# Agent attention with a cosine feed-forward: a PSUM bank of its own for the output products, the program order kept on four engines, and the side work laid out by hand in half lots

## The chip, the cores and the metric

One core of a Trainium2 chip runs the kernel. The metric is the device time of one execution in microseconds (us). The engines are TensorE (PE in the profile, PEld for its weight loads), VectorE (DVE), ScalarE (ACT), GpSimd (POOL) and SyncE (SP), which issues the DMAs.

## The reference

Four batches of 12480 tokens with 128 channels, 49 agents, and a feed-forward of 2048 columns:

```
scale = 1 / sqrt(128)
sm(a, b) = softmax over the last axis of scale * (a @ b.T)
agent_v = sm(agents, k) @ v              # 49 x 128 per batch
x       = sm(q, agents) @ agent_v        # 12480 x 128 per batch
h       = x @ w_in                       # 49920 x 2048
out     = (h * cos(h)) @ w_out           # 49920 x 128
```

All of it is in float32. The kernel folds agent_v @ w_in into one matrix `a` per batch (`project`), so that h is softmax weights times `a`, and it computes h * (cos(h) - 1) and adds the linear part x @ w_in @ w_out by two short products (`project_out`, b1 and b2).

## The kernel before

**Work and names.** A group is 960 tokens (8 tiles of 120), 13 groups make a batch, 52 the whole. The feed-forward of a group takes two halves of 480 tokens with eight steps each, so 16 steps a group, 208 a batch (called a stretch here) and 832 in all, in the loop at line 512. One step n has four parts: two products on PE (L520) that fill a tile `ph` of two PSUM banks (three such tiles); the sine on ACT (L523) from `ph` to `c`, with the bias read from a tile `half_pi`; on DVE (c - 1) * h (L525) into `r`; and, four steps later (LAG), two products of `r` with w_out on PE (L542) that add up over eight steps in one PSUM bank. At the end of the eight come the two linear products (L538, L539), and ACT copies the bank to `osb` (L544), from where SP writes the output.

**Side work.** While the loop runs over one batch, the next batch is prepared, and so are the softmax weights of the groups that come. The side work goes by lots, one group each: a key lot (`Agents.scores`: eight products, L93, then an ACT copy L171 and a running maximum on DVE, L182), a query lot (`query`: eight products, L93, then DVE takes the maximum, L342, and subtracts it, L349), a values lot (`values`: eight products, L232). An fp32 product is two matmuls in the trace, so a lot of eight shows as 16. A query group is turned by four transposes (`query_turned`, L372, ACT copy L374, POOL L377 and L378). `Agents.shift` subtracts the maximum on POOL (L210). Once the keys and queries of a batch are in, ACT changes its function table from sine to exponential, takes the exponentials of all 13 key lots (three instructions, L214) and of all 13 query groups (three instructions, L353), and changes back: this is a burst. DVE then sums the queries' exponentials (`query_sums`, L357 to L359). Batch 0 has two small bursts of five groups, batches 1 to 3 a large one each.

**What sets the order.** All these one-bank results (scores, turned weights, the output products) come from one pool `p1` of two PSUM banks (`small`, the name `one` in the profile). `extra` gives a lot to a whole step, steps 1, 3 and 5 of eight; the lots of the next batch follow one another as early as they can, all keys, then all queries, then the burst, then all values. Only some instructions are pinned (`tc.keep_in_program_order`); the rest is put in order on each engine by a list scheduler.

Of the kernel before, what the change touches and what calls it, by code (L numbers as in the profile page):

```python
# [18 lines left out]
P = 128  # L19
# [16 lines left out]
LAG = 4  # L36
PAD = 64
# [4 lines left out]
def agent_attention_cos_ffn(ctx, tc, qT, kT, v, agT, w_in, w_out, outT):  # L42
# [15 lines left out]

    const = ctx.enter_context(tc.tile_pool(name="const", bufs=1))
# [4 lines left out]
    nc.gpsimd.memset(ones, 1.0)  # L64
    half_pi = const.tile([P, 1], F32, name="half_pi")
    nc.gpsimd.memset(half_pi, HALF_PI)
# [20 lines left out]
    def scores(sb, src, b, ps):  # L87

        xt = sb.tile([P, GRP], F32, name="xt", bufs=3)
        load(xt, src)  # L90
        ps = ps[:TT, :GT * NA].rearrange("p (t a) -> p t a", a=NA)
        for t in range(GT):
            nc.tensor.matmul(ps[:, t, :], xt[:, t * TT:(t + 1) * TT], ag[:, b, :], start=True, stop=True)  # L93
        return ps

    def scores_twice(xt, src, b, ps):
# [3 lines left out]
        for t in range(GT):  # L100
            nc.tensor.matmul(ps[:, t // HT, t % HT], xt[:, t * TT:(t + 1) * TT], twice(ag[:, b, :]),  # L101
                             start=True, stop=True)
        return ps[:, :, :, 0, :]

    class Weights:
# [6 lines left out]
        def single(self, src, out):  # L112
# [5 lines left out]
            nc.vector.tensor_scalar(ex, hi, 20, 0x7FF, op0=ALU.logical_shift_right, op1=ALU.bitwise_and)  # L118
            nc.vector.tensor_scalar(man, hi, 0xFFFFF, 0x100000, op0=ALU.bitwise_and, op1=ALU.bitwise_or)
            nc.vector.tensor_scalar(ex, ex, 1151.0, 896.0, op0=ALU.min, op1=ALU.max)  # L120
            f = man.bitcast(F32)
            nc.vector.scalar_tensor_tensor(f, lo, 2.0 ** -32, man, op0=ALU.mult, op1=ALU.add)
            nc.vector.tensor_scalar(ex, ex, 896.0, 2.0 ** 23, op0=ALU.subtract, op1=ALU.mult)
            nc.vector.scalar_tensor_tensor(f, f, 2.0 ** -20, ex.bitcast(F32), op0=ALU.mult, op1=ALU.mult)
            nc.vector.scalar_tensor_tensor(out.bitcast(U32), hi, 0x80000000, man, op0=ALU.bitwise_and, op1=ALU.bitwise_or)
# [5 lines left out]
        def w_out(self, c):  # L131
# [3 lines left out]
            nc.scalar.copy(w1[:, fs], w)  # L135
            return w

        def product(self, c, w, po, wio):

            pt = self.psum()  # L140
            for t in range(4):
                f = slice((4 * c + t) * P, (4 * c + t + 1) * P)
                nc.tensor.transpose(pt[:, t * P:(t + 1) * P], win[:, f], ident)
            wt = self.sb.tile([P, 4, P], F32, name="wt", bufs=2)
            nc.scalar.copy(wt.rearrange("p f d -> p (f d)"), pt)
            for t in range(4):
                nc.tensor.matmul(po, wt[:, t], w[:, t], start=(c == t == 0), stop=(4 * c + t == NF - 1))
            if 4 * c + 4 == NF:
                nc.vector.tensor_copy(wio, po)

    class Agents:
# [6 lines left out]
        def scores(self, g):  # L158
            sb = self.sb
            if g == 0:  # L160
# [5 lines left out]
                nc.gpsimd.memset(av[:, NA:HI], 0.0)  # L166
# [3 lines left out]
            if self.wide is None:  # L170
                nc.scalar.copy(s, scores(sb, src, self.b, self.psum()))  # L171
            else:
# [5 lines left out]
                nc.scalar.copy(s.rearrange("p (h t) a -> p h t a", h=2), ps)  # L178
            if g == 0:
                nc.vector.tensor_copy(self.run, s)  # L180
            else:
                nc.vector.tensor_max(self.run, self.run, s)  # L182
# [41 lines left out]
        def values(self, g):  # L224
            vt = self.sb.tile([TT, GT, P], F32, name="vt", bufs=4)
# [468 lines left out]
```

## Time and profile before

| | us |
|---|---|
| median of three timed runs (1282.61 to 1286.02) | 1284.95 |
| span of the profiled execution | 1283.9 |
| PE, PEld busy | 1188.2, 955.3 |
| DVE, ACT, POOL busy | 1087.6, 1005.6, 313.8 |

The span runs from the first to the last instruction of the profiled execution, and is the only time of that execution that is given; the median of the timed runs lies 1.05 above it. PE's busy time counts each matmul from its start to its modelled end, and pipelined matmuls overlap, so that how much of PE is used is read from the distance of starts, not from the busy share. The first output step's DVE instruction starts at 86.9, the last at 1274.8; ahead of that stand the loading of the weights and the keys and values of batch 0.

### The profile page before, as it was taken

How to read it: one execution, taken by the hardware profiler on the slowest of the kernel's cores; microseconds unless marked ns; L12 is line 12 of the kernel's file. 1: busy time of each engine (PE TensorE's matmuls, PEld its weight loads, DVE VectorE, ACT ScalarE, POOL GpSimd, SP SyncE). 2: the span in 40 equal slices, each digit the busy share in tenths (PEclk: the TensorE clock that was granted, in tenths of full speed). 3: DMA queues.
4: the chain of work that ended last, by engine and by line, in shares of the span. 5: the costliest groups of instructions: out<-in, count | busy, mean ns of one | idle time of the engine just before them, and what ended most of it. 6: DMA issues, size and time to landing. Idle time of an engine off the chain costs nothing.

```text
span 1283.9 us, 17193 instructions
## 1 busy us (share of the span) xinstructions
PE 1188.2 (93%) x6349; PEld 955.3 (74%) x6349; DVE 1087.6 (85%) x1214; ACT 1005.6 (78%) x1115; POOL 313.8 (24%) x341
## 2 busy tenths in 40 slices
PE   8799899996999999969999999996999999999997
PEld 8777787775987887758966788775986666666664
DVE  5878778887779888878799988787789999999997
ACT  2347778667779887676799988667789999999997
POOL 1201221415213115133132121415133122222220
PEclk9989999998999999999999999998999999999999
DMA  8953333331440342324400133331500000000000
GB/s 301 247 153 111 92 108 108 93 109 61 109 108 31 108 131 70 108 77 108 133 22 31 54 116 93 108 93 31 136 19 32 31 16 31 31 31 16 31 31 34
DMA packets 31016, 107.72 MB, mean 84 GB/s; under 512 B 3436, under 2 KB 3820, under 8 KB 30924
## 3 DMA queue, kind: packets, MB, share of 16 engines
q1 hardware_dynamic: 30924, 106.54, 27.3%
q8 instruction: 52, 0.85, 0.3%
q14 instruction: 40, 0.33, 0.1%
HBM read 80.97 MB, written 25.56 MB: 83 GB/s over the span
## 4 chain that ended last, share of the span: by engine, by line
PE 56%; ACT 17%; DVE 15%; issue 7%; POOL 2%; DMA 2%; ACTq 0%; SPq 0%; POOLq 0%
PE ph L520 19%; PE one L542 14%; DVE r L525 13%; PE one L93 11%; ACT c L523 11%; PE one L232 5%; ACT osb L544 2%; PE ph L101 2%; DMA vt<-v 1%; PE ph L232 1%; PE one L538 1%; PE one L539 1%; DVE mx L342 1%; ACT e L353 1%; PE one L372 1%
## 5 line engine op out<-in xcount | busy, mean ns | idle before, releaser
L525 DVE SCALAR_TENSOR_TENSOR r<-c,ph 128x960 fp32r<-128x960 f32 x832 | 922.6, 1149 | 109.0 <-ACT c L523 104.2
L523 ACT ACTIVATE c<-ph,half_pi 128x960 f32<-128x960 f32 x832 | 859.3, 1068 | 198.6 <-PE ph L520 185.5
L520 PE MATMUL ph<-pT,a 113*128 113x480 f32 x1664 | 542.5, 407 | 33.2 <-DVE r L525 30.3
L542 PE MATMUL one<-r,w 128*128 128x480 f32 x1664 | 515.9, 389 | 3.9 <-ACT osb L544 2.8
L520 PEld LDWEIGHTS ph<-pT,a 113*128 113x128 f32 x1664 | 282.2, 190 | 167.6 <-DVE r L525 86.7
L542 PEld LDWEIGHTS one<-r,w 128*128 128x128 f32 x1664 | 308.1, 190 | 49.4 <-ACT osb L544 4.0
L363 POOL TENSOR_TENSOR p<-e,rz 120x392 f32<-120x392 f32 x52 | 44.9, 864 | 767.4 <-PE one L372 681.2
L93 PEld LDWEIGHTS one<-ag,xt 128*120 128x120 f32 x1408 | 164.1, 184 | 21.9 <-ACT osb L544 11.9
L93 PE MATMUL one<-ag,xt 128*120 128x49 f32 x1408 | 163.6, 265 | 2.5 <-ACT osb L544 0.6
L378 POOL TENSOR_TENSOR pT<-p,pT 49x480 fp32r<-49x480 f32 x104 | 127.1, 1222 | 8.0
L232 PE MATMUL one<-s,vt 120*128 120x98 f32 x624 | 80.6, 284 | 27.9 <-ACT osb L544 27.7
L232 PEld LDWEIGHTS one<-s,vt 120*128 120x128 f32 x624 | 80.2, 202 | 32.0 <-ACT osb L544 29.0
L377 POOL CAST pT<-p 49x480 fp32r<-49x480 f32 x104 | 61.4, 591 | 52.2 <-ACT p L374 48.9
L544 ACT COPY osb<-one 128x480 f32<-128x480 f32 x104 | 57.8, 556 | 2.7 <-PE one L542 2.7
L342 DVE TENSOR_REDUCE mx<-one 120x8 f32<-120x392 f32 x49 | 27.5, 562 | 32.2 <-PE one L93 32.2
L372 PEld LDWEIGHTS one<-ident,p 120*113 120x113 f32 x208 | 30.2, 179 | 22.3 <-ACT osb L544 16.5
L372 PE MATMUL one<-ident,p 120*113 120x120 f32 x208 | 37.3, 281 | 7.5 <-ACT osb L544 5.1
L538 PE MATMUL one<-pT,b 113*128 113x480 f32 x104 | 39.9, 383 | 0.0
L539 PE MATMUL one<-pT,b 113*128 113x480 f32 x104 | 39.8, 382 | 0.0
L357 DVE TENSOR_REDUCE rz<-e 120x32 f32<-120x1568 f32 (+2 forms) x12 | 22.7, 1916 | 18.2 <-ACT e L353 18.2
L210 POOL TENSOR_TENSOR s<-s,mxb 120x1568 f32<-120x1568 f32 (+1 forms) x9 | 31.4, 3522 | 26.9 <-DVE mxb L206 26.9
L222 POOL TENSOR_TENSOR es<-es,s 120x392 f32<-120x392 f32 x36 | 36.7, 1018 | 2.8
(91 smaller groups left out, 504.0 us busy)
## 6 DMA issues: line engine op xcount, KB each, us to landing
xt<-qT SPq DMA_DIRECT2D x52, 480.0 KB, 3.4
vt<-v SPq DMA_DIRECT2D x52, 480.0 KB, 4.3
outT<-osb SPq DMA_DIRECT2D x51, 480.0 KB, 2.5
xt<-kT SPq DMA_DIRECT2D x46, 480.0 KB, 3.5
c<-kT SPq DMA_DIRECT2D x6, 480.0 KB, 6.6
raw<-w_in SPq DMA_DIRECT2D x4, 512.0 KB, 5.7
raw<-w_out SPq DMA_DIRECT2D x4, 512.0 KB, 10.9
outT<-osb SPq DMA_DIRECT2D x2, 240.0 KB, 2.0
```

The costliest lines, as they stand in the source:

```text
L93: nc.tensor.matmul(ps[:, t, :], xt[:, t * TT:(t + 1) * TT], ag[:, b, :], start=True, stop=True)
L232: nc.tensor.matmul(po, vt[:, t, :], twice(e[:, t, :]), start=(t == 0 and (g == 0 or not lone)), stop=(t == GT - 1 and (g == NG - 1 or not ...
L372: nc.tensor.transpose(pt[:KR, t * TT:(t + 1) * TT], p_in[n % 2][:, t, :KR], ident[:TT, :TT])
L377: nc.gpsimd.tensor_copy(pT[own, c], p[own])
L378: nc.gpsimd.tensor_sub(pT[other, c], p[own], pT[own, c].bitcast(F32))
L520: nc.tensor.matmul(ph[:, j, :CH], ai[:, f], pTs[q % 3][:, c], start=True, stop=True)
L523: nc.scalar.activation(cos, h, AF.Sin, bias=half_pi, scale=1.0)
L525: nc.vector.scalar_tensor_tensor(r, cos, 1.0, h, op0=ALU.subtract, op1=ALU.mult)
L538: nc.tensor.matmul(po, b1[k], pTs[q % 3][:, c], start=False, stop=False)
L539: nc.tensor.matmul(po, b2[k], pTs[q % 3][:, c], start=False, stop=False)
L542: nc.tensor.matmul(po, w1[:, f, :], r[:, j, :], start=(f == 0), stop=(f == NF - 1))
L544: nc.scalar.copy(osb[:, c * CH:(c + 1) * CH], po)
```

## The change

Every operation on PE, DVE, ACT and POOL goes through a wrapper (`Ordered`) that pins it to the order in which the program writes it while the loop runs, so the profile of the changed kernel has one line (L88) for all of them. The output products get a bank of their own (`po`), and `small` has one bank left instead of two. Key, query and values lots are cut in two halves of four products, one half to a step, in six of eight steps. Query scores are made some 16 to 100 steps ahead of their use and no longer all ahead of one burst: a stretch has two bursts, the first (step 120) with the keys' exponentials and six queries', the second (step 8 of the next stretch) with seven queries'. A burst has the scores of two more query groups in it (`query_two`, in a `ph` tile), and the first has five values lots. Exponentials and sums of queries go group by group. The sine's bias is a constant. The sine's reader on DVE comes behind the step's side work. Cut to its core:

```diff
+        def __getattr__(self, op):
...
+                if looping[0]:
+                    tc.keep_in_program_order(ins)
...
+    pe, dve, act, pool = (Ordered(x) for x in (nc.tensor, nc.vector, nc.scalar, nc.gpsimd))
...
+    def part_scores(half, src, b, k):
...
+        for t in range(k * HT, (k + 1) * HT):
+            pe.matmul(ps[:, t, :], xt[:, t * TT:(t + 1) * TT], ag[:, b, :], start=True, stop=True)
+        return ps if k else None
...
-        ps_1 = pools.enter_context(tc.tile_pool(name="p1", bufs=2, space=PSUM))
+        ps_1 = pools.enter_context(tc.tile_pool(name="p1", bufs=1, space=PSUM))
...
+        ps_o = pools.enter_context(tc.tile_pool(name="po", bufs=1, space=PSUM))
...
+        def query_two(two, piece):
+            ps = pair()[:TT, :, :GT * NA]
...
         def query_exp(piece):
-            tc.keep_in_program_order(nc.scalar.activation(e_of[piece], e_of[piece], AF.Exp, scale=SC))
...
+            for n in piece:
+                tc.keep_in_program_order(act.activation(e_of[n], e_of[n], AF.Exp, scale=SC))
+        def query_sum(n):
+            dve.reduce_sum(rz_of[n], e_of[n], axis=AX.X)
...
-            while n in taken or (n - LAG) % NP not in (1, 3, 5):
+            while at in shut or (at - LAG) % NP not in SLOTS:
...
+        def burst(n, piece, two=(), ab=None):
+            shut.update(range(n, n + 4))
+            if two:
+                post(n, query_two, two, piece_of[two[0]])
+            if ab is not None:
+                for g, k in lots:
+                    post(n, pinned_exp, ab, g, k)
+                for g in range(NV):
+                    plan(n + 3, ab.values, g, None, (0, NV - 1))
...
+            post(n, query_exp, piece)
...
+            burst(go, early[b], two_of(late[b]), nxt)
+            spread_over(go + 4, o + V1, o + V1, [[(nxt.values, g, k) for k in range(2)] for g in range(NV, NG)])
...
+            burst(stop, late[b], two_of(early[b + 1]))
...
-                nc.scalar.activation(cos, h, AF.Sin, bias=half_pi, scale=1.0)
+                act.activation(cos, h, AF.Sin, bias=HALF_PI, scale=1.0)
+            plan.run(n)
+            if n < NSTEP:
                 r = rs[n] = sb.tile([P, 2, CH], F32R, name="r", bufs=6)
-                nc.vector.scalar_tensor_tensor(r, cos, 1.0, h, op0=ALU.subtract, op1=ALU.mult)
-            plan.run(n)
+                dve.scalar_tensor_tensor(r, cos, 1.0, h, op0=ALU.subtract, op1=ALU.mult)
+            post.run(n)
...
-                po = small()[:, :CH]
+                po = ps_o.tile([P, 512], F32, name="po")[:, :CH]
```

Three places show what moved. In the rows x8 and the like count equal instructions in a row, and a row's last figures are the result's shape.

First, PE where key lots are made (`one<-ag,xt`), some 70 steps into the loop before, and 20 steps into the second stretch in the changed order. Before:

```order
L520 MATMUL ph<-pT_88,a_82 128x480 x2
L542 MATMUL one<-r,w_70 128x480
L93 MATMUL one<-ag,xt 120x49 x8
L542 MATMUL one<-r,w_70 128x480
L538 MATMUL one<-pT_90,b_84 128x480
L520 MATMUL ph<-pT_88,a_82 128x480 x2
```

Now:

```order
L88 MATMUL ph<-pT_93,a_86 128x480 x2
L88 MATMUL one<-ag,xt 120x49 x4
L88 MATMUL po<-r,w_70 128x480 x2
L88 MATMUL ph<-pT_93,a_86 128x480 x2
L88 MATMUL one<-ag,xt 120x49 x4
L88 MATMUL po<-r,w_70 128x480 x2
```

A lot of eight stood in one piece between the output products of a step; now four products stand behind each step's `ph` and ahead of its output products, which go to `po`.

Second, the large burst on ACT in the second stretch (`s` are the keys' scores, `e` the queries'). Before:

```order
L523 ACTIVATE c<-ph,half_pi 128x960 x8
L214 ACT_TABLE_LOAD
L214 ACTIVATE s<-s 120x1568
L374 COPY p<-one 113x480
L214 ACTIVATE s<-s 120x1568
L214 ACTIVATE s<-s 120x1960
L353 ACTIVATE e<-e 120x1568 x2
L353 ACTIVATE e<-e 120x1960
L523 ACT_TABLE_LOAD
```

Now the same burst on ACT, and under it what PE does from the step of the burst on:

```order
L88 ACTIVATE c<-ph 128x960 x4
L88 ACT_TABLE_LOAD
L88 ACTIVATE s<-s 120x1568 x2
L88 ACTIVATE s<-s 120x1960
L88 ACTIVATE e<-e 120x392 x6
L88 ACT_TABLE_LOAD
L88 ACTIVATE c<-ph 128x960 x3
```

```order
L88 MATMUL ph<-pT_93,a_86 128x480 x2
L88 MATMUL ph<-ag,xt 120x49 x16
L88 MATMUL po<-r,w_70 128x480 x2
L88 MATMUL ph<-pT_93,a_86 128x480 x2
L88 MATMUL po<-r,w_70 128x480 x2
L88 MATMUL ph<-pT_93,a_86 128x480 x2
L88 MATMUL po<-r,w_70 128x480 x2
L88 MATMUL ph<-pT_93,a_86 128x480 x2
L88 MATMUL one<-s,vt 128x2x49 x40
L88 MATMUL po<-pT_93,b_88 128x480
```

The burst has six query groups where it had thirteen, and PE has two query lots and five values lots (x40) in it.

Third, DVE around query lots, `mx` the maximum and `e` the difference. Before:

```order
L525 SCALAR_TENSOR_TENSOR r<-c,ph 128x960 x5
L342 TENSOR_REDUCE mx_2505<-one 120x8
L525 SCALAR_TENSOR_TENSOR r<-c,ph 128x960
L349 TENSOR_TENSOR e<-one,mx_2505 120x392
L525 SCALAR_TENSOR_TENSOR r<-c,ph 128x960
```

Now:

```order
L88 TENSOR_TENSOR run<-run,s 120x392
L88 SCALAR_TENSOR_TENSOR r<-c,ph 128x960 x3
L88 TENSOR_REDUCE mx_4165<-one 120x8
L88 TENSOR_TENSOR e<-one,mx_4165 120x392
L88 SCALAR_TENSOR_TENSOR r<-c,ph 128x960 x3
L88 TENSOR_TENSOR run<-run,s 120x392
```

The two steps of a query lot stand together, with no step of the loop between them.

## Rows read from the trace of the kernel before

**Rows 1.** The run by windows: before the loop, three of the four stretches of 208 steps (left out is the third, 308.40 us, like the second), and the end. The figure behind the window is its length. Behind each engine stand its busy us and its instructions, then the granted TensorE clock.

```profile
0.00:86.90 86.90, 73.58 (x537) 68.65 (x537) 60.81 (x122) 25.52 (x45) 12.58 (x25) 0.92 0.86 254
86.90:421.70 334.80, 309.31 (x1746) 257.25 (x1747) 276.53 (x314) 257.91 (x281) 83.34 (x87) 0.97 0.31 92
421.70:731.20 309.50, 290.26 (x1577) 235.82 (x1576) 261.35 (x285) 248.48 (x274) 83.45 (x86) 0.98 0.28 83
...
1039.60:1274.80 235.20, 223.68 (x928) 158.65 (x926) 226.09 (x208) 225.05 (x245) 51.15 (x58) 1.00 0.07 29
1274.80:1283.90 9.10, 1.87 (x7) 1.05 (x7) 1.68 (x5) 0.56 (x1) 0.00 (x0) 0.67 0.12 38
```

**Rows 2.** PE's timeline where key lots are made (start, length, tiles): plain steps and a lot of 16.

```profile
442.96 0.61 PE L520 MATMUL ph<-pT,a 113*128 113x480 f32 x2
443.40 1.78 PE L93 MATMUL one<-ag,xt 128*120 128x49 f32 x16
...
445.53 0.60 PE L520 MATMUL ph<-pT,a 113*128 113x480 f32 x2
...
446.63 0.59 PE L520 MATMUL ph<-pT,a 113*128 113x480 f32 x2
447.06 0.38 PE L539 MATMUL one<-pT,b 113*128 113x480 f32 x1
...
447.72 0.60 PE L520 MATMUL ph<-pT,a 113*128 113x480 f32 x2
```

**Rows 3.** PE's timeline where values lots are made: a lot of 16.

```profile
330.18 0.60 PE L520 MATMUL ph<-pT,a 113*128 113x480 f32 x2
...
330.83 1.92 PE L232 MATMUL one<-s,vt 120*128 120x98 f32 x16
...
332.84 0.60 PE L520 MATMUL ph<-pT,a 113*128 113x480 f32 x2
```

**Rows 4.** Groups of instructions by line and shape, over the whole run: count, then busy us and mean ns of one, then the idle time ahead of them and what ended it.

```profile
L523 ACT ACTIVATE c<-ph,half_pi 128x960 f32<-128x960 f32 x832 | 859.3, 1068 | 198.6 <-PE ph L520 185.5 <-DVE r L525 1.9 <-DVE mxb L206 1.3
L342 DVE TENSOR_REDUCE mx<-one 120x8 f32<-120x392 f32 x49 | 27.5, 562 | 32.2 <-PE one L93 32.2
L349 DVE TENSOR_TENSOR e<-one,mx 120x392 f32<-120x392 f32 x49 | 27.4, 559 | 0.0
L266 ACT ACTIVATE a<-one,rz 113x512 fp32r<-113x512 f32 x16 | 11.2, 697 | 1.9 <-PE one L263 1.8
L145 ACT COPY wt<-one 128x512 f32<-128x512 f32 x4 | 2.4, 588 | 22.2 <-PE one L143 22.2
L214 ACT ACTIVATE s<-s 120x392 f32<-120x392 f32 x13 | 6.6, 527 | 5.8 <-DVE s L210 5.8
```

**Rows 5.** The large burst of the second stretch: ACT's timeline, DVE's, and PE's (in brackets the idle time before and what ended it).

```profile
562.27 1.06 ACT L523 ACTIVATE c<-ph,half_pi 128x960 f32<-128x960 f32 x1 [1.72 <-PE ph L520]
563.35 1.28 ACT L214 ACT_TABLE_LOAD   x1
564.64 1.51 ACT L214 ACTIVATE s<-s 120x1568 f32<-120x1568 f32 x1
...
566.50 3.24 ACT L214 ACTIVATE s<-s 120x1568 f32<-120x1568 f32 x2
569.64 4.62 ACT L353 ACTIVATE e<-e 120x1568 f32<-120x1568 f32 x3
574.28 1.28 ACT L523 ACT_TABLE_LOAD   x1
575.58 1.06 ACT L523 ACTIVATE c<-ph,half_pi 128x960 f32<-128x960 f32 x1
...
563.35 2.21 DVE L525 SCALAR_TENSOR_TENSOR r<-c,ph 128x960 fp32r<-128x960 f32 x2
...
576.90 1.14 DVE L525 SCALAR_TENSOR_TENSOR r<-c,ph 128x960 fp32r<-128x960 f32 x1
...
577.14 3.73 PE L232 MATMUL one<-s,vt 120*128 120x98 f32 x16 [8.90 <-ACT osb L544]
```

**Rows 6.** Windows of 32 steps of the loop where key lots, query lots and values lots stand closest, and a window behind the burst; columns as in rows 1. Under them, for the same first three windows, the matmuls of L93 (first two rows) and of L232 (last row) alone, on PE and PEld.

```profile
445.10:492.50 47.40, 46.66 (x265) 38.47 (x265) 40.12 (x45) 39.25 (x46) 8.96 (x10) 1.00 0.35 105
492.50:547.40 54.90, 51.56 (x309) 42.73 (x308) 44.18 (x53) 36.78 (x39) 19.28 (x13) 1.00 0.32 100
334.50:381.70 47.20, 47.20 (x292) 42.65 (x291) 36.93 (x41) 34.31 (x39) 9.10 (x11) 1.00 0.45 124
571.40:581.60 10.20, 4.46 (x19) 4.32 (x20) 10.20 (x12) 7.57 (x7) 9.41 (x11) 0.50 0.00 1
...
445.10:492.50 47.40, 13.46 (x113) 13.53 (x112) 1.00 0.35 105
492.50:547.40 54.90, 18.10 (x160) 18.11 (x160) 1.00 0.32 100
...
334.50:381.70 47.20, 16.96 (x143) 16.95 (x141) 1.00 0.45 124
```

**Rows 7.** Waits: who waited for whom, us in total, how often, the longest. The first row is from the last stretch alone (1039.6 to 1274.8), the others from the whole run.

```profile
DVE r L525 <- ACT c L523: 8.8, 38, 0.3
...
PEld one L372 <- ACT osb L544: 16.5, 27, 0.7
PEld one L93 <- ACT osb L544: 11.9, 24, 0.7
```

More of the change, by code (lines that the diff above doesn't have):

```diff
@@ L36 @@
 LAG = 4
+SLOTS = [0, 2, 3, 4, 5, 6]
+S0 = 24
+T1 = 120
+T2 = 8
+K1 = 84
+V1 = 180
+NV = 5
+WL = 16
+TL = 13
+SH = 2
+AD = 2
+KB = 16
+SF = 2
+SA = 4
+SD = 4
 PAD = 64
@@ L227, in values @@
             lone = self.wide is not None
-            if g == 0 or not lone:
+            first, last = (0, NG - 1) if lone else run or (g, g)
+            if g == first and not k:
                 self.po = self.copies(self.wide()[:, 0] if lone else self.psum())
             e, po = self.part(g), self.po
-            for t in range(GT):
-                nc.tensor.matmul(po, vt[:, t, :], twice(e[:, t, :]), start=(t == 0 and (g == 0 or not lone)),
-                                 stop=(t == GT - 1 and (g == NG - 1 or not lone)))
@@ L234, in values @@
-            if g == (NG - 1 if lone else 0):
-                nc.vector.tensor_copy(self.sums, po)
-            elif not lone:
-                nc.vector.tensor_add(self.sums, self.sums, po)
+            for t in range(GT) if k is None else range(k * HT, (k + 1) * HT):
+                pe.matmul(po, vt[:, t, :], twice(e[:, t, :]), start=(t == 0 and g == first),
+                                 stop=(t == GT - 1 and g == last))
+            if k != 0 and g == last:
+                self.gather(first, po)
@@ L330, in agent_attention_cos_ffn, with query @@
         e_of, rz_of = {}, {}
-        PIECES = 5
-        def query(n, piece, wide=False):
+        PIECES = 7
+        half = dict(sb=sb, psum=small)
+        def query(n, k, piece, wide=False):
             b, g = n // NG, n % NG
@@ L349, in query @@
[L349 to L359 removed]
+            dve.reduce_max(mx, ps, axis=AX.X)
@@ new lines, in query @@
+            room(piece)
+            dve.tensor_sub(e_of[n].rearrange("p (h t) a -> p h t a", h=2), ps,
+                           mx.unsqueeze(3).to_broadcast([TT, 2, HT, NA]))
+        def query_two(two, piece):
+            ps = pair()[:TT, :, :GT * NA]
+            for j, n in enumerate(two):
+                xt = sb.tile([P, GRP], F32, name="xt", bufs=3)
+                load(xt, qT[n // NG, :, n % NG * GRP:(n % NG + 1) * GRP])
+                for t in range(GT):
+                    pe.matmul(ps[:, j, t * NA:(t + 1) * NA], xt[:, t * TT:(t + 1) * TT], ag[:, n // NG, :], start=True, stop=True)
+            ps = ps.rearrange("p j (t a) -> p j t a", a=NA)
+            mx = sb.tile([TT, 2, GT], F32, name="mx3", bufs=1)
+            dve.reduce_max(mx, ps, axis=AX.X)
+            room(piece)
+            i = piece.index(two[0])
+            dve.tensor_sub(whole[piece][:, i * GT:(i + 2) * GT].rearrange("p (j t) a -> p j t a", j=2), ps,
+                           mx.unsqueeze(3).to_broadcast([TT, 2, GT, NA]))
@@ L403, in agent_attention_cos_ffn @@
         pre(NG, ab[0].across)
-        for n in pieces[0][0]:
-            pre(NG, query, n, pieces[0][0], True)
+        for n in pieces[0]:
+            pre(NG, query, n, 0, pieces[0], True)
         pre(NG, ab[0].spread)
@@ new lines, in agent_attention_cos_ffn @@
+        at = 0
+        while queue:
+            while at in shut or (at - LAG) % NP not in SLOTS:
+                at += 1
+            ready = [x for x in queue if x[0] <= at]
+            if not ready:
+                at += 1
+                continue
+            x = min(ready, key=lambda x: (x[2], x[1]))
+            queue.remove(x)
+            n, _, by, parts = x
+            for f, *args in parts:
+                while at in shut or (at - LAG) % NP not in SLOTS:
+                    at += 1
+                plan(at, f, *args)
+                at += 1
```

336 lines of the change are left out of this document (191 added, 145 removed).

## The prediction

> **What bounds the kernel now.** I read the run by windows first [rows 1]. The time falls into 86.9 us before the loop, stretches of 334.8, 309.5, 308.4 and 235.2 us of 208 steps each, and an end of 9.1. Each stretch does the same 208 steps; the first three also prepare the next batch. In the last one DVE is busy 226.1 of 235.2 us, 1.087 a step: it is bound by DVE. In the second DVE is busy 261.4 of 309.5, so 48 us go elsewhere.
>
> The busy share of PE says little, so I price its work by distances of starts. From one `ph` to the next, with one linear product between (0.22), 446.63 to 447.72, is 1.09: a plain step is 0.87 [rows 2]. With a lot of 16 between, 442.96 to 445.53 is 2.57: a score lot adds 1.70 [rows 2]. The same with a values lot is 2.66: 1.79 [rows 3]. The linear products add 0.43 in eight steps; four transposes at the score matmul's 1.70/16 are 0.42 a group. So a step with these is 0.87 + 0.054 + 0.026 = 0.95. The second stretch is 208 x 0.95 = 197.6, 26 score lots 44.2, 13 values lots 23.3, and 2 for the projection (eight matmuls of 512 columns): 267 us of PE work in 309.5. DVE has 261. Both engines have nearly the same work, and 42 us are lost because they don't have it at the same time.
>
> Where the 42 go:
> - The burst. ACT leaves the sine from 563.35 to 575.58; DVE's last product ends at 565.56 and the next starts at 576.90, and PE sits idle for 8.9 [rows 5].
> - The clock behind it. In 571.4 to 581.6 the granted clock is 0.50, so 1.2 of 2.4 GHz, after that idle PE; 16 values matmuls take 3.73 there against 1.92 later [rows 3, 5, 6]. Half of 10.2 us is 5.
> - Lots in heaps. Where query lots stand closest, 32 steps take 54.9 against PE work of 32 x 0.95 + 10 x 1.70 = 47.4, a loss of 0.23 a step; where keys do, 47.4 against 30.4 + 7.1 x 1.70 = 42.4, 0.16 a step; with values 47.2 against 30.4 + 8.9 x 1.79 = 46.4, 0.03 [rows 6] (its matmul counts by 16 give the lots).
> - After them, DVE and ACT bind the steps while PE has 0.95 of work in 1.13.
>
> **The change, part by part.**
> *Spreading the lots.* The order now has 13 key and 3 query lots in steps 12 to 84 of a stretch, one query lot to step 120, eight values and 3.5 query lots in steps 124 to 180, then the projection. I take for each piece the engine with more work.
> - Steps 0 to 12 with the second burst: DVE 12 x 1.087 + 2.2 (maximum and difference of the two groups; at most 2 x 1.12 by [rows 4]) + 1.5 for sums = 16.7, and 2.3 idle: ACT is away for two table loads and seven exponentials, 2.56 + 7 x 0.43 = 5.6 (0.527 less the 0.1 by which neighbours overlap) [rows 4, 5], and DVE has 3.3 to do meanwhile. 19.0.
> - 72 steps: PE 68.4 + 16 x 1.70 = 95.6 (DVE some 92).
> - 36 steps: DVE 39.1 + 1.1 + 2 = 42.2.
> - Four steps with the first burst. ACT is away 2.56 + 4.6 (keys) + 2.6 = 9.8. PE meanwhile does two query lots 3.4, three steps of `ph` and output 2.6, then five values lots 8.9 and the next step 1.4: 16.3, without a gap, so the piece is PE's and its idle time is filled. The clock should stay at 1.00.
> - 56 steps: PE 53.2 + 6.0 + 14.3 = 73.5.
> - 28 steps: DVE 30.4 + 1.1 + 3.7 = 35.2.
>
> Sum 281.8. First stretch: 26 steps with three projections and six query lots, DVE 38.3 plus 4 for the chain at the start; 58 steps with 16.5 lots and a small burst, 85; then as above, 42.2 + 16.3 + 73.5 + 35.2: 294.5. Last stretch: 208 x 1.087 = 226.1, and on DVE four query groups 4.4, sums and inverses 6, two bursts' idle 5.3: 241.8, so 6.6 more than before for work that stood earlier.
>
> *What is still lost.* New is how DVE and PE meet. The bounds are 0.03 a step (values) and 0.23 (queries) [rows 6]. I take 0.05 for the first three stretches, 31 us: queries are now one lot in about 16 steps, and DVE waits for half a lot at most, where it waited for whole ones (32.2 us in all) [rows 4]. For the last I take 0.02, 4 us: it lost 0.044, 8.8 us of it by waits for ACT [rows 7], and ACT gets shorter.
>
> *The sine's bias.* An ACT instruction of 512 columns from PSUM with a tile operand takes 697 ns, one without 588 [rows 4]; so the sine's 1068 should become about 959. It frees ACT by about 90 us in all. If nothing changes here, ACT stays as it is, and some 10 us of the 0.02 and 0.05 come back.
>
> *Exponentials by group, two bursts.* Six more table loads in the loop, 6 x 1.28 = 7.7 us of ACT, and shorter exponentials, 49 x about 0.07 = 3.5 (thirteen groups took 4.62 in three); both are in the bursts above. At 563.35 the load starts 0.02 after the sine's end, and the exponential 0.01 after the load's [rows 5]. The Trainium skill (ScalarE: Activation LUTs, What ACT_TABLE_LOAD costs) puts a switch at about 2.66 us, with 1.38 for a drain besides the load; by it the six would cost another 8.3 us of ACT, which speaks against two bursts. The rows above have no such gap, and the sum stays.
>
> *Pinning, POOL's subtractions in 13 pieces, DMAs.* POOL is busy 83 of 309.5 [rows 1]; the groups' weights come 16 steps ahead now. Bytes and loads are the same. Nothing for either; if a load came late, PE would show it.
>
> **Sum.** 86.9 + 294.5 + 2 x 281.8 + 241.8 + 9.1 + 31 + 4 = 1231 against the span of 1283.9, so 53 less. The median of the runs lies 1.05 above the span: **1232**.
>
> **The rivals.**
> - *The engines meet better.* With a loss of 0 to 0.02 a step the sum is 1196 to 1212. For it: values lots, which nobody on DVE reads until the end, lose only 0.03. Against: DVE still reads every key and query lot. 1200.
> - *The gain is half lost again.* 0.09 to 0.13 a step, between the values and the key window. For it: 0.16 with keys in a two-bank pool [rows 6], and 13 keys still stand in 72 steps. 1255 to 1281, say 1265.
> - *One bank for all side results (slower).* Each key, query, turned and values lot must now wait until the last one's reader is done, and on PE everything pinned behind it waits too, the next `ph` in front. Before, such waits were 0.50 and 0.61 us each, with two banks [rows 7]. A stretch has some 52 handovers; at 0.6 us each that is 31 us, 0.15 a step, and the gain is gone; at the 1.12 of both DVE readers [rows 4] it is 58, and the run takes 1196 + 3 x 58 + 4 = 1374; at 0.8, 1325. Against: two steps of a lot stand in different steps, and between most lots lie output products and `ph`, 0.87, which cover the wait. The Trainium skill (Perfetto Trace Analysis, Optimizing Tensor Performance) tells one to rotate independent matmul groups through different banks so that reading one overlaps the next; by that rule this rival is the likely one. The waits above agree that a handover costs, but not that often. The point from which it decides is 0.6 us at each handover.
> - *The change doesn't do what it says.* The bursts idle PE as before, or the sine stays at 1068: 10 to 25 us more than forecast, inside the range.
>
> **Chances.** Forecast (1212 to 1255) 0.45; meets better 0.20; half lost 0.20; no change (within 0.3%, 4 us, about what a measurement can tell) 0.05; slower 0.10. So faster 0.85. The range leaves out a little of the best case, the worst of the half-lost one, no change and slower: 1188 to 1274.
>
> **What would show it.** Stretches of about 305, 292, 292 and 246 us. Sine near 960 ns. PE's granted clock 1.00 through the large bursts, with five values lots running while ACT is at exponentials. DVE busy about 0.9 of the loop. PE's waits for DVE or ACT on tile `one` below 0.3 us a lot. It is wrong if PE waits on `one` at most lots (slower rival), if the last stretch exceeds 255 (DVE's order stalls), or if the first three stay above 300.

## The result and the profile after

The changed kernel takes 1239.74 us (median of four runs, 1239.28 to 1241.23) beside 1285.49 for the kernel before: a ratio of 0.9647, interval 0.963 to 0.9664. Its profiled execution takes 1239.28, its span is 1237.5. The forecast was 1232, the range 1188 to 1274.

By windows, cut as in [rows 1] (ahead of the loop, the four stretches, the end; busy us and instructions of PE, PEld, DVE, ACT, POOL, then the granted clock, the share of the DMA engines and GB/s):

```profile
0.00:85.90 85.90, 70.06 (x531) 65.32 (x531) 57.35 (x120) 24.84 (x45) 10.23 (x21) 0.94 0.87 257
85.90:394.20 308.30, 296.61 (x1671) 247.57 (x1669) 270.56 (x308) 235.19 (x287) 85.48 (x97) 0.99 0.31 92
394.20:685.70 291.50, 284.32 (x1575) 236.57 (x1575) 261.52 (x289) 234.05 (x286) 86.01 (x97) 1.00 0.30 89
685.70:984.30 298.60, 291.40 (x1576) 243.72 (x1575) 262.51 (x289) 234.35 (x286) 85.91 (x97) 0.97 0.26 80
984.30:1229.00 244.70, 233.18 (x993) 172.86 (x993) 234.36 (x234) 219.64 (x260) 52.56 (x59) 0.98 0.08 30
1229.00:1237.50 8.50, 1.77 (x6) 0.97 (x6) 1.50 (x4) 0.56 (x1) 0.00 (x0) 0.75 0.14 40
```

DVE does the same 261 us in the second stretch as before, but in 291.5 us and not 309.5. The first three stretches are 26.5, 18.0 and 9.8 shorter; the last, which has taken over a query burst and four query groups, is 9.5 longer.

The second stretch by the pieces of the forecast (steps 0 to 12 with the second burst; 72 steps with key lots; 36 without; 4 with the first burst; 56 with values lots; 28 behind), columns as above, and in the last row a window behind the second burst of the third stretch, 704.2 to 717.9:

```profile
394.20:412.60 18.40, 16.58 (x93) 13.60 (x94) 16.29 (x19) 17.50 (x24) 4.47 (x6) 1.00 0.26 81
412.60:512.30 99.70, 98.78 (x576) 84.82 (x576) 90.77 (x100) 78.12 (x99) 18.80 (x20) 1.00 0.33 100
512.30:554.80 42.50, 40.60 (x186) 30.20 (x185) 41.18 (x43) 36.82 (x44) 23.69 (x27) 1.00 0.13 46
554.80:571.60 16.80, 16.80 (x133) 15.93 (x133) 8.05 (x12) 13.54 (x16) 5.15 (x6) 1.00 0.66 174
571.60:649.90 78.30, 76.99 (x442) 66.87 (x440) 70.68 (x80) 57.43 (x68) 22.60 (x25) 1.00 0.37 103
649.90:685.70 35.80, 34.56 (x152) 25.15 (x152) 34.56 (x40) 30.63 (x38) 11.29 (x14) 1.00 0.11 39
704.20:717.90 13.70, 13.70 (x49) 12.17 (x48) 10.18 (x15) 5.58 (x7) 0.00 (x0) 0.50 0.25 72
```

The forecast had 19.0, 95.6, 42.2, 16.3, 73.5, 35.2 ahead of its loss. The two long pieces that PE bounds are clearly longer, by 4.1 in 72 steps (0.057 a step) and 4.8 in 56 (0.086); the other four lie within 0.6. The second stretch has no time at half clock (a granted clock of 0.50, so 1.2 of 2.4 GHz); the third has 17.1 us of it and is 7.1 longer.

The large burst of the second stretch on ACT and on PE, to set beside [rows 5] (start, length, in brackets idle time before):

```profile
554.50 1.28 ACT L88 ACT_TABLE_LOAD   x1
555.79 4.64 ACT L88 ACTIVATE s<-s 120x1568 f32<-120x1568 f32 x3
560.34 2.61 ACT L88 ACTIVATE e<-e 120x392 f32<-120x392 f32 x6
562.96 1.28 ACT L88 ACT_TABLE_LOAD   x1
564.26 2.69 ACT L88 ACTIVATE c<-ph 128x960 f32<-128x960 f32 x3
...
553.83 3.56 PE L88 MATMUL ph<-ag,xt 128*120 128x49 f32 x32 [0.36 <-DVE r L88]
...
560.15 9.07 PE L88 MATMUL one<-s,vt 120*128 120x98 f32 x80
569.00 0.68 PE L88 MATMUL po<-pT,b 113*128 113x480 f32 x2
```

ACT is away from 554.50 to 564.26, 9.8 us where it was 12.2. PE, idle for 8.9 in the same place before, has query lots and five values lots (x80) and no gap.

Groups and waits of the whole run, beside [rows 4] and [rows 7]. First the groups,

```profile
L88 DVE SCALAR_TENSOR_TENSOR r<-c,ph 128x960 fp32r<-128x960 f32 x832 | 912.2, 1149 | 52.1 <-ACT c L88 51.2
L88 ACT ACTIVATE c<-ph 128x960 f32<-128x960 f32 x832 | 788.7, 973 | 207.8 <-PE ph L88 189.5
```

and who waited for whom (us in all, times, longest):

```profile
PEld po L88 <- ACT osb L88: 21.7, 34, 2.6
PE po L88 <- ACT osb L88: 8.1, 29, 2.2
DVE mx L88 <- PE one L88: 5.2, 12, 2.1
PE one L88 <- DVE e L88: 1.9, 4, 0.5
```

The sine went from 1068 to 973 ns, and DVE's wait for query scores in `one` from 32.2 to 5.2 us; another 11.5 are waits in the bursts, for the scores of two groups in a `ph` tile. PE waits little for the readers of `one`: the waits of weight loads for them in the loop are 11.5 us in all. It does wait for the copy of the output products to leave `po`: at 34 of the handovers from one half to the next, with 21.7 us on the weight loads and, at 29 of the same 34, 8.1 on the products behind them.

### The profile page after: what moved, and what is told of

The parts are those of the page before. It is cut to its first block, busy times and chain, and to the rows that moved or that the text cites. A ratio compares the mean times of both kernels' runs of the same rounds, so it can differ in the third digit from the quotient of the medians.

```text
span 1237.5 us, 17245 instructions
## 1 busy us (share of the span) xinstructions
PE 1177.3 (95%) x6349; PEld 967.0 (78%) x6349; DVE 1087.8 (88%) x1238; ACT 948.6 (77%) x1161; POOL 320.2 (26%) x371
## 4 chain that ended last, share of the span: by engine, by line
PE 63%; DVE 19%; ACT 11%; issue 3%; DMA 3%; SPq 0%; ACTq 0%
PE ph L88 26%; PE po L88 22%; DVE r L88 15%; PE one L88 15%; ACT c L88 7%; DMA vt<-v 2%; ACT osb L88 1%; ACT p L88 1%; DVE e L88 1%; DVE mx L88 1%; DVE rz L88 1%; ACT s L88 1%; DVE run L88 1%; DMA c<-kT 1%; ACT e L88 0%
## 5 line engine op out<-in xcount | busy, mean ns | idle before, releaser
L88 DVE SCALAR_TENSOR_TENSOR r<-c,ph 128x960 fp32r<-128x960 f32 x832 | 912.2, 1149 | 52.1 <-ACT c L88 51.2
L88 ACT ACTIVATE c<-ph 128x960 f32<-128x960 f32 x832 | 788.7, 973 | 207.8 <-PE ph L88 189.5
L88 PE MATMUL ph<-pT,a 113*128 113x480 f32 x1664 | 528.1, 399 | 21.7 <-DVE r L88 16.3
L88 PE MATMUL po<-r,w 128*128 128x480 f32 x1664 | 535.9, 404 | 8.4 <-ACT osb L88 8.1
L88 PEld LDWEIGHTS ph<-pT,a 113*128 113x128 f32 x1664 | 299.9, 191 | 140.7 <-DVE r L88 75.4
L88 PEld LDWEIGHTS po<-r,w 128*128 128x128 f32 x1664 | 295.1, 192 | 59.5 <-ACT osb L88 21.7
L88 POOL CAST pT<-p 49x480 fp32r<-49x480 f32 x104 | 60.4, 581 | 742.0 <-ACT p L88 738.9
L88 PEld LDWEIGHTS one<-ag,xt 128*120 128x120 f32 x1184 | 148.9, 188 | 19.0 <-PE ph L88 3.7
L88 PE MATMUL one<-ag,xt 128*120 128x49 f32 x1184 | 143.0, 264 | 4.5 <-PE ph L88 1.8
L88 POOL TENSOR_TENSOR pT<-p,pT 49x480 fp32r<-49x480 f32 x104 | 126.8, 1219 | 8.3
L88 PEld LDWEIGHTS one<-s,vt 120*128 120x128 f32 x624 | 77.6, 192 | 3.1
L88 PE MATMUL one<-s,vt 120*128 120x98 f32 x624 | 76.6, 271 | 0.0
L88 POOL TENSOR_TENSOR p<-e,rz 120x392 f32<-120x392 f32 x52 | 47.1, 907 | 87.9 <-DVE rz L88 85.8
L88 ACT COPY osb<-po 128x480 f32<-128x480 f32 x104 | 58.1, 559 | 13.3 <-PE po L88 13.3
L88 PE MATMUL po<-pT,b 113*128 113x480 f32 x208 | 62.3, 381 | 0.0
L88 PE MATMUL ph<-ag,xt 128*120 128x49 f32 (+1 forms) x384 | 45.9, 279 | 7.5 <-DMA xt<-kT 5.3
L88 DVE TENSOR_TENSOR run<-run,s 120x392 f32<-120x392 f32 x48 | 28.5, 594 | 27.0 <-ACT s L88 26.7
L88 PEld LDWEIGHTS ph<-ag,xt 128*120 128x120 f32 x384 | 44.3, 195 | 10.1 <-issue 5.5
L88 PEld LDWEIGHTS po<-pT,b 113*128 113x128 f32 x208 | 38.8, 188 | 6.1
L88 POOL TENSOR_TENSOR s<-s,mxb 120x392 f32<-120x392 f32 x39 | 36.4, 965 | 12.1 <-DVE mxb L88 11.6
L88 POOL TENSOR_TENSOR es<-es,s 120x392 f32<-120x392 f32 x36 | 37.0, 1028 | 2.4
L88 ACT COPY p<-one 113x480 f32<-113x480 f32 x52 | 29.5, 567 | 8.0 <-PE one L88 7.9
```

The source lines that it names most:

```text
L88: ins = f(*args, **kw)
```

## The experiments

Times of the stretches are from each kernel's trace (first DVE product of one stretch to that of the next); "half" is the time in the loop at a granted clock of 0.50, so 1.2 of 2.4 GHz. The ratio is against the kernel before, run on the same chip; its medians there lie between 1282.9 and 1285.5, so medians of different rows can be set side by side to about 3 us.

| kernel | median (lowest to highest) | ratio, interval | ahead of loop; stretches 1 to 4 | half |
|---|---|---|---|---|
| before | 1284.95 (1282.61 to 1286.02) | | 86.9; 334.8, 309.5, 308.4, 235.2 | 37.5 |
| after | 1239.74 (1239.28 to 1241.23) | 0.9647, 0.963 to 0.9664 | 85.9; 308.3, 291.5, 298.6, 244.7 | 31.2 |
| after_again | 1240.26 (1237.48 to 1241.41) | 0.9656, 0.9638 to 0.9675 | 89.9; 310.4, 294.4, 291.6, 245.0 | 30.6 |
| bias_tile | 1257.77 (1250.01 to 1267.36) | 0.9803, 0.9755 to 0.985 | 88.3; 316.9, 295.5, 296.7, 250.2 | 37.6 |
| bias_only | 1271.07 (1267.08 to 1274.24) | 0.9894, 0.9863 to 0.9924 | 83.2; 331.9, 307.2, 306.1, 230.7 | 47.9 |
| no_fill | 1255.8 (1248.89 to 1262.47) | 0.9758, 0.9712 to 0.9804 | 91.0; 316.9, 299.1, 300.5, 244.9 | 54.6 |
| heaped | 1251.78 (1246.92 to 1264.53) | 0.9764, 0.9708 to 0.9819 | 90.8; 312.8, 296.4, 296.3, 245.7 | 17.5 |
| whole_lots | 1262.46 (1261.4 to 1262.9) | 0.984, 0.9822 to 0.9859 | 88.5; 318.9, 301.3, 299.8, 244.2 | 25.1 |
| unpinned | 1273.09 (1271.43 to 1276.1) | 0.9927, 0.9907 to 0.9948 | 84.1; 315.0, 306.1, 304.4, 250.7 | 40.9 |
| shared_bank | 1225.34 (1223.18 to 1229.16) | 0.9542, 0.9522 to 0.9562 | 84.0; 306.4, 293.3, 293.3, 241.6 | 37.5 |
| bank_only | 1275.47 (1273.82 to 1276.58) | 0.9943, 0.9924 to 0.9963 | 82.5; 333.5, 313.3, 296.7, 236.8 | 34.1 |
| late_fill | 1250.66 (1245.65 to 1251.61) | 0.9732, 0.9706 to 0.9757 | 89.8; 317.9, 298.7, 298.4, 236.6 | 28.1 |
| key_fill | 1229.26 (1225.38 to 1238.36) | 0.9604, 0.9572 to 0.9636 | 82.9; 306.3, 293.2, 294.6, 240.2 | 20.4 |
| longer_keys | 1230.18 (1228.68 to 1236.0) | 0.9583, 0.9557 to 0.9609 | 85.4; 309.0, 293.7, 293.6, 241.6 | 33.9 |

Second stretch by the six pieces, from the same starts (half clock in brackets where there is any):

| kernel | 0-12 | 12-84 | 84-120 | 120-124 | 124-180 | 180-208 |
|---|---|---|---|---|---|---|
| after | 18.4 | 99.7 | 42.5 | 16.9 | 78.3 | 35.8 |
| after_again | 18.4 | 99.6 | 42.5 | 19.8 (6.8) | 78.3 | 35.8 |
| bias_tile | 19.0 | 101.0 | 43.3 | 16.9 | 79.0 | 36.2 |
| no_fill | 18.4 | 99.7 | 42.5 | 13.9 (4.8) | 88.8 (5.4) | 35.8 |
| heaped | 18.4 | 102.5 | 41.1 | 16.9 | 83.1 | 34.5 |
| whole_lots | 21.1 (6.8) | 103.8 | 42.5 | 17.8 | 80.2 | 36.0 |
| unpinned | 21.9 (3.1) | 103.0 (3.7) | 42.7 | 23.7 (5.3) | 77.4 (1.6) | 37.4 |
| shared_bank | 19.7 (6.8) | 99.4 | 42.2 | 18.2 (3.4) | 78.3 | 35.5 |
| late_fill | 18.1 | 95.9 | 42.8 | 16.8 | 76.6 | 48.4 (6.8) |
| key_fill | 18.7 | 100.3 | 42.2 | 18.2 (3.4) | 78.3 | 35.5 |
| longer_keys | 19.7 (6.8) | 98.4 | 44.9 | 16.9 | 78.3 | 35.5 |

**after_again**, the changed kernel once more.

> The changed kernel once more, beside the next three. In the four runs before this, kernels that differ little varied by 10 to 20 us from run to run, and their traces put it down to where the granted clock is at 0.50: ahead of the loop and behind the second bursts. Theory (the clock falls there in this kernel too, only not in every run): 1238 to 1250, and a trace whose stretches, taken without the time at half clock, are those of the first trace (291.5 without a fall). Rival (the kernel itself is steady): 1239 to 1242 again.

The time is steady, 1240.26. The trace is not: half clock lies in other places. Pieces without it agree within 0.1 us between the two traces, so pieces are the finer measure, and the medians of kernels that spread by 14 to 18 us (bias_tile, no_fill, heaped) are read with them.

**bias_tile and bias_only**, the sine's bias from a tile in the changed kernel, and as a constant in the kernel before.

```diff
-                act.activation(cos, h, AF.Sin, bias=HALF_PI, scale=1.0)
+                act.activation(cos, h, AF.Sin, bias=half_pi, scale=1.0)
```

> The changed kernel with the sine's bias read from a tile again. Theory: the constant bias takes 95 ns off a sine (1068 to 973), so the sine goes back to about 1070; PE or DVE bind the first three stretches, so little of the 832 x 0.095 = 79 us comes back: about 7 us in the last stretch (244.7 to about 252, where DVE waits for ACT at light steps of 1.09 a step) and about 1 to 3 in all the others together, so 8 to 10 us in all: 1248 to 1250. Rival A: ACT is hidden everywhere once the order is fixed: under 3 us, about 1241. Rival B: ACT at 0.80 busy is what sets how well PE and DVE meet (a sine that comes later holds a product and a buffer): 20 us or more, 1260 and up.

> The kernel before with the sine's bias as a constant and nothing else. Theory: sine 1068 to about 973; the last stretch, where DVE waits for ACT 8.8 us, falls from 235.2 to 227 to 229; the first three, where PE's lots and the burst set the time, by 0 to 2 each; in all 6 to 12 us off the time of the kernel before, 1273 to 1279. Rival (ACT bound more than the waits say): 20 us or more off. Rival (bias read from a tile is hidden): within 2 us.

The sine is back at its old size:

```profile
L88 ACT ACTIVATE c<-ph,half_pi 128x960 f32<-128x960 f32 x832 | 861.6, 1068 | 156.1 <-PE ph L88 146.7
```

It costs 18 us by medians. In the second stretch, without half clock in either, it is 4.0, spread over five of six pieces (0.6, 1.3, 0.8, 0.7, 0.4); in the last it is 5.5. In the kernel before the constant alone brings 12.8, a little over the theory's 6 to 12. The theory's part on the last stretch holds roughly (5.5 for about 7, and 4.5 for 6 to 8 in the kernel before). That the first three hide it falls: a sine that ends later gives its result and its `ph` buffer later also where PE bounds. In the second stretch DVE's waits for the sine grow from 12.6 to 14.7 us, and PE's for a free `ph` from 16.3 to 17.8 on weight loads and from 3.9 to 6.3 on products. The size lies between the theory and rival B.

**no_fill**, one values lot instead of five in the first burst.

```diff
-NV = 5
+NV = 1
```

> The changed kernel with one values lot instead of five in the first burst of each stretch (the other four go to the 56 steps behind it). Theory: PE has 3.4 + 2.6 + 1.8 us of work in the 9.8 us that ACT is away and is idle for some 3 to 5, and the 7.1 us of values work lies in the PE-bound steps behind, which grow from 78.3 to about 84; together 5 to 8 a stretch, and where the granted clock falls to 0.50 behind the idle PE another 5: plus 16 to 36 us over three stretches, 1256 to 1276. Rival (the burst costs what ACT is away, whatever PE does, because DVE has the rest to do): under 4 us in all, 1240 to 1244.

Plus 16 by medians, the low end of the theory. In the second stretch the burst's piece is 3.0 shorter and the values' piece 10.5 longer, 7.5 in all, with 10.2 us of half clock; the changed kernel has none there in one trace and 6.8 in the other. The burst's fill is work taken off a piece that PE bounds.

**heaped and whole_lots**, lots as early as their slots allow, and both halves of a lot in one step.

```diff
-                job(lo + (hi - lo) * i / len(jobs), *parts, by=...)
+                job(lo, *parts, by=...)
```

```diff
-                at += 1
+                if len(parts) != 2 or (f, args) != (parts[0][0], list(parts[0][1:])):
+                    at += 1
```

> The changed kernel with the lots of each piece started as early as their slots allow instead of evenly spread over it (13 key lots from step 12 in some 35 steps instead of 72, eight values lots in some 22 instead of 56). Theory of the prediction: heaps lose 0.16 a step (keys) where spread lots lose 0.06, and behind them steps are bound by DVE at 1.09 while PE has 0.95: about 4 to 8 us more a stretch, 12 to 24 in all: 1252 to 1264. Rival (half lots, the order and the bank are what count, and by the sum of bounds it is the same where in the piece the lots stand: 35 steps of PE at 55 and 37 of DVE at 41 are 96 against 95.6): within 4 us, 1236 to 1244.

> The changed kernel (output products in their own bank, 1240 us) with both halves of a lot in one step, everything else the same. Theory: a step with a whole lot is 0.95 + 1.70 = 2.65 us on PE while DVE needs 1.09, and the three buffers of ph cover about two steps of it; the keys' piece loses 0.10 a step more (0.16 as in the kernel before against 0.06), 7 us a stretch, the queries 1 to 2 more: 15 to 27 in all, 1255 to 1267. Rival (the buffers cover whole lots, since two lots stand at least four steps apart now): within 4 us, 1236 to 1244.

heaped is 12 slower by medians, at the low edge of its theory; its second stretch is 4.9 longer with no half clock: keys 2.8, values 4.8, and 1.4 and 1.3 less in the pieces behind. whole_lots is 22 slower, as its theory has it, but not all where it has it: the keys' piece is 4.1 longer and not 7, the values' piece 1.9, the burst's 0.9. The rivals fall. Who waits in whole_lots (first row PE for a free `ph`, then the readers of whole lots; in the changed kernel these rows have 80.0, 0.5 and 5.2 us):

```profile
PEld ph L88 <- DVE r L88: 108.3, 237, 4.0
ACT s L88 <- PE one L88: 27.4, 39, 1.5
DVE mx L88 <- PE one L88: 14.6, 28, 1.2
```

**unpinned**, the wrapper pins nothing.

```diff
-                if looping[0]:
+                if False:
                     tc.keep_in_program_order(ins)
```

> The changed kernel with no instruction pinned by the wrapper (the few that the kernel before pins stay), so that the list scheduler puts the same work in order on each engine; it joins the halves of a lot to whole lots of eight and moves output products. Theory: the spreading and the bursts come from the steps that the work is given to, the pins only keep them; the scheduler's joined lots lose as whole lots did (0.16 a step against 0.06 in 72 steps of keys: 7 us a stretch): 10 to 30 us more, 1250 to 1270. Rival A (the pins are cosmetic): 1236 to 1244. Rival B (most of the gain is the kept order): 1275 or more.

Plus 33 us, above the theory's 10 to 30 and near rival B: of the single undoings the dearest. The dearest place is the large burst, 23.7 against 16.9 us (5.3 of it at half clock). ACT, DVE and PE there:

```profile
576.15 2.70 ACT L88 ACTIVATE c<-ph 128x960 f32<-128x960 f32 x3
...
589.32 0.97 ACT L88 ACTIVATE c<-ph 128x960 f32<-128x960 f32 x1 [7.89 <-PE ph L88]
...
583.05 0.81 DVE L88 TENSOR_REDUCE es<-es 120x49 f32<-120x392 f32 x1 [7.20 <-POOL es L88]
...
584.99 3.26 DVE L88 SCALAR_TENSOR_TENSOR r<-c,ph 128x960 fp32r<-128x960 f32 x3
...
585.13 3.31 PE L88 MATMUL one<-s,vt 120*128 120x98 f32 x14 [4.29 <-DVE av L88]
```

Three sines are done by 578.85, but the scheduler has put the sum of the keys' weights (`es`, due at step 180) ahead of their products on DVE, and it waits 7.20 for POOL. So `ph` is not freed, and ACT has nothing for 7.89. The kept order prevents just that. This place costs 6.8 us a stretch, half clock included; the rest of the 33 lies mostly in the first two pieces (3.5 and 3.3 in the second stretch, again with some half clock).

**shared_bank and bank_only**, output products and side results in two common banks in the changed kernel, and in banks of their own in the kernel before.

```diff
-        ps_1 = pools.enter_context(tc.tile_pool(name="p1", bufs=1, space=PSUM))
+        ps_1 = pools.enter_context(tc.tile_pool(name="p1", bufs=2, space=PSUM))
-                po = ps_o.tile([P, 512], F32, name="po")[:, :CH]
+                po = small()[:, :CH]
```

> The changed kernel with the output products back in the pool of the side results, two banks for both, the order kept. Theory: with the order kept on PE the output products hold one of the two banks for eight steps and the lots the other, as with banks of their own; the bank by itself brings 0 to 8 us: 1239 to 1250. Rival (the bank is what lets the half lots run: a lot must wait for the copy of the output products, as the waits of 0.50 and 0.61 us a lot in the kernel before): 52 handovers a stretch at 0.5 to 0.6 us, 26 to 31 us a stretch, 80 to 90 in all: 1320 or more; waits of PE for osb on the tile of the lots by the hundred.

> The kernel before with a bank of its own for the output products and one bank for the side results, nothing else. Theory (from shared_bank: a bank of its own costs a wait for the copy at each of 104 handovers of the output products, 12 to 15 us): in this kernel it costs that too, and whole lots and turned weights that stand one behind the other now share one bank: 10 to 45 us more, 1293 to 1328. Rival (a bank of its own frees the lots of the waits for the output copy, 16.5 + 11.9 + 29 us in the kernel before): 5 to 25 us less, 1258 to 1278.

Neither expectation for shared_bank had the right sign: without the bank of its own the kernel is faster by 15 us, 0.9542 against 0.9656 on the same chip, and beats both kernels. The handover between one half's output products and the next is the place. First the changed kernel, in the last stretch:

```profile
1094.67 0.60 PE L88 MATMUL po<-r,w 128*128 128x480 f32 x2
1095.11 0.59 PE L88 MATMUL ph<-pT,a 113*128 113x480 f32 x2
1095.92 0.70 PE L88 MATMUL po<-r,w 128*128 128x480 f32 x2 [0.22 <-ACT osb L88]
```

Then shared_bank, the same step:

```profile
1086.40 0.60 PE L88 MATMUL one<-r,w 128*128 128x480 f32 x2
1086.84 0.61 PE L88 MATMUL ph<-pT,a 113*128 113x480 f32 x2
1087.28 0.59 PE L88 MATMUL one<-r,w 128*128 128x480 f32 x2
```

With one bank the next product starts 0.81 behind `ph`, with two 0.44: 0.37 less. Not every handover gains this. Of the 103 in the loop only 32 have nothing but a `ph` between the two halves' products; 43 have four transposes there as well, which take the second bank in shared_bank, and the others half lots or the projection, and in nearly all of these the distance is the same in both kernels. Over all 103 the times from the last product of one half to the first of the next add up to 126.3 and 124.7 us in the two traces of the changed kernel and to 113.9 in shared_bank, so some 11 to 12 us less. The waits for `osb` fall from 21.7 and 8.1 us (weight loads and products) to 5.4 and 2.9:

```profile
PEld one L88 <- ACT osb L88: 5.4, 8, 2.6
PE one L88 <- ACT osb L88: 2.9, 4, 2.2
```

Of the 15 us the traces show 3.1 in the last stretch, 1.9 in the first, and 0.9 in the second's pieces without half clock; with half clock and all, the loop is 7 to 9 us shorter. The part ahead of the loop takes 82.9 to 85.4 in three traces with two banks for side results and 85.9 to 91.0 in seven with one and the order kept. But the three have 6.8 us of half clock there and the seven 9.7 to 27.0, and unpinned, with one bank and 6.8, takes 84.1; so that this part is the bank's is not shown. The traced run of shared_bank is also the slowest of its four (1229.16 against a median of 1225.34). In the kernel before the bank brings 7 us, the opposite sign and the rival's, though its waits for `osb` are long:

```profile
PEld po L543 <- ACT osb L545: 72.0, 75, 5.2
PE po L543 <- ACT osb L545: 43.5, 56, 5.0
```

There the scheduler makes another order with it, so what the bank itself does is not told apart.

**late_fill, key_fill and longer_keys**, tries to better it. late_fill is the changed kernel, the others build on shared_bank.

```diff
-T2 = 8
+T2 = -24
+NL = 10
...
+            if last is not None:
+                for g in range(NL, NG):
+                    plan(n + 3, last.values, g, None, (NL, NG - 1))
```

> The changed kernel with the second burst at step 184 of the same stretch instead of step 8 of the next, and three values lots (10 to 12) in it, so that PE has work while ACT is at the seven exponentials; keys start at step 2 of a stretch. Theory (PE idle in the second burst, 1.3 to 3 us, is what the granted clock falls behind, 7 us where it does): no half clock behind the second bursts in the stretches, loss at the keys smaller since they have 82 steps instead of 72; 5 to 20 us less than the changed kernel beside it. Rival A (the burst's cost is DVE's idle time, the same wherever it stands; the values lots make PE late for the projection): within 4 us. Rival B (the projection comes late and the next stretch waits): 5 us or more slower.

The projection also starts six steps later here. The kernel is 10 us slower (rival B's size). Steps 180 to 208, which now hold the burst, take 48.4 instead of 35.8; the keys give back 3.8 and the values 1.7, and the last stretch, rid of its second burst, some 8. PE is at the three lots when the sine is back, and DVE, whose addition of their sum (`av`) stands ahead of the step's own product, waits for their end:

```profile
675.97 0.26 DVE L89 TENSOR_TENSOR av<-av,one 128x98 f32<-128x98 f32 x1 [5.16 <-PE one L89]
676.15 1.15 DVE L89 SCALAR_TENSOR_TENSOR r<-c,ph 128x960 fp32r<-128x960 f32 x1
```


```diff
+            if b + 2 < NB:
+                for k in range(2):
+                    plan(stop + 3, ab[b + 2].scores, 0, k)
```

> The changed kernel with two banks shared by output products and side results (1225 us), and besides with the first key lot of the batch after next whole in the second burst of stretches 2 and 3, where PE has room for one lot of 1.7 us (late_fill's three lots of 5.4 were more than the room). Theory: PE is busy through the burst, the granted clock stays at 1.00 behind it (two falls of 6.8 us, 3.4 us lost by each), and the keys' PE-bound piece has one lot less: 2 to 5 us a stretch in two stretches: 1216 to 1222. Rival (the lot stands between the burst and the steps that DVE waits for, and takes as much there as it gives elsewhere): 1223 to 1230.

No gain, 0.9604 against 0.9542: of shared_bank's falls of the granted clock at the second bursts, those of stretches 2 and 4 are gone in its trace, though only stretches 2 and 3 got a lot, and that of stretch 3 is there (6.8 us). It begins at 692.6, ahead of the added lot (699.55), so the lot can't have kept it off. Steps 0 to 12 of the second are 1.0 shorter, the keys' piece 0.9 longer. The rival's size holds.

```diff
-K1 = 84
+K1 = 96
...
-SH = 2
+SH = 1
```

> The changed kernel with two banks shared by output products and side results (1225 us), and besides with the key lots spread to step 96 instead of 84 and POOL's subtractions one step apart instead of two, so that they still end ahead of the burst at step 120. Theory (the prediction's sum by pieces: each piece lasts as long as the engine with more work there): steps 12 to 84 are bound by PE and steps 84 to 120 by DVE; 84 steps with the same lots take 84 x 0.95 + 16 x 1.70 = 107 and the 24 steps behind 28.2, in all 135.2, where it is now 95.6 + 42.2 = 137.8: 2.6 a stretch less, 8 us in all: 1215 to 1220. Rival A (the loss per step is what counts, and it grows with the length of the piece in which both engines are nearly full): within 3 us, 1222 to 1229. Rival B (POOL's subtractions come late and the keys' exponentials wait in the burst): 1230 or more.

The median, 1230.18, lies just beyond rival A's range and at the edge of rival B's, but the trace speaks for A: the burst of the second stretch is as long as in the changed kernel (16.9), so the keys' exponentials don't wait. Steps 12 to 84 fall by 1.0 only, steps 84 to 120 grow by 2.7. A sum of each piece's larger engine promised 2.6 less for the two together.

## Why the prediction came out

- **Stretches.** Forecast 305, 292, 292, 246; measured 308.3, 291.5, 298.6, 244.7. The second stretch loses 9.8 us against the sum of its pieces, 0.047 a step for the 0.05 that was taken. But the loss was spread evenly in the forecast, and it lies nearly all in the two long PE-bound pieces (0.057, 0.086). In part the total is luck: of the 4 us allowed in the last stretch for how the engines meet, 3.1 are the bank's, since shared_bank takes 241.6 there. The sign "the first three stay above 300" can't have meant the first, for which the forecast itself had 305.
- **Bursts.** ACT away 9.8 and 5.7 us (forecast 9.8 and 5.6), PE without a gap in the first. The load of the table stands 0.01 ahead of the exponentials (554.50 + 1.28 to 555.79), and no load in the traces before and after has more than 0.02 us idle ahead of it and 0.17 behind. The 1.38 us of drain that the Trainium skill (ScalarE: Activation LUTs, What ACT_TABLE_LOAD costs) adds to a switch show nowhere, as [rows 5] said.
- **Clock: half right.** It should stay at 1.00 through the large bursts; in two traces it did in four of six. The falls at the small second bursts were not in the forecast (four in the six of the stretches 2 to 4 of both traces), and the third stretch, with 17.1 us at half clock, is the one that misses clearly (298.6 for 292).
- **The sine's bias: undersized.** The sine itself fell less than priced (to 973 ns, not 959), but "some 10 us" were 18 (12.8 in the kernel before), because it counts in the first three stretches too.
- **Pinning: wrong.** "Nothing" was the price of pinning; without it 33 us are lost. The forecast took the new order as given and never priced what the scheduler would do with it.
- **The own bank: not priced, and a loss.** The sum had no term for it. The slower rival asked the right question at the wrong tile: handovers of `one` cost little, those of `po` cost 0.37 us where only a `ph` lies between (32 of 103). With the bank the kernel is 15 us slower, not 93; some 12 us stand at the handovers, and not all of that reaches the time of the loop. By the rule of the Trainium skill (Perfetto Trace Analysis, Optimizing Tensor Performance) independent matmul groups should rotate through different banks. shared_bank, where the output products of one half and the next can, bears it out (waits of weight loads for `osb` 5.4 us for 21.7).
- **Spreading, halves, fill: right in sign.** Undone alone they cost 12, 22 and 16 us. With 18 and 33 the single undoings add to 101, over twice the 46 us gained, so they don't add up; that they share the same waits is likely but not shown. Three parts were not undone by themselves: the second burst, the scores of two query groups in a burst, and DVE's reader of the sine behind the side work.

## What to carry to other kernels

When two engines are nearly full, price the pieces by the larger engine plus a loss per step. The loss can grow as they are balanced better, and moving work further then brings nothing (one run here, longer_keys). Look for handovers of a single accumulation bank, where products stand one behind the other, before giving it a bank of its own. Order is a cost too: one reduction that waits for a slow engine, ahead of urgent work, stops its own engine and two others (7.20 us on DVE, 7.89 on ACT, 4.29 on PE in unpinned).

## What the runs showed that was not expected

The granted clock can fall with PE busy. In after_again it is 0.51, the lower of its two levels (1.2 of 2.4 GHz), from 562.6 to 569.5, and PE was busy 10.18 of the 10.60 us ahead of it:

```profile
552.00:562.60 10.60, 10.18 (x59) 8.15 (x58) 9.86 (x10) 10.17 (x12) 4.54 (x5) 1.00 0.12 46
562.60:569.50 6.90, 6.90 (x24) 6.06 (x24) 3.41 (x6) 6.88 (x10) 2.33 (x3) 0.51 0.51 145
```

The first trace of the same program, with the same products in the same place, stays at 1.00. The fall cost 3.0 us there (19.8 against 16.8), near half of its 6.9; at a second burst, where DVE bounds, 6.8 us of it cost 1.3 (the changed kernel's fourth stretch, 19.7 against 18.4 in its second, which has none). The falls at shared_bank's second bursts are of this kind too: they begin at 400.4, 694.0 and 987.5, at most 1.9 us after ACT's table load and with no gap of PE above 0.4 in the burst up to there. What decides it stays open. key_fill and late_fill don't answer it: the lots that they add for PE (from 699.55 and 670.02) start behind the beginning of the falls that are left at the second bursts there (692.6 and 664.1).
